# A third unit of the second chunk by 32x32 squares and VectorE transposes, with its loads and the loads of v on GpSimd's queue

## The chip, the cores and the metric

The program runs on one core of a Trainium2 chip. The metric is the device time in microseconds (us). Three timed runs of the kernel before gave 600.76, 600.92 and 600.96 us; their median is 600.92 us. One further execution was profiled; it took 601.11 us, of which the profile's span covers 599.4 us.

Engines are named as in the profile: PE (TensorE matmuls), PEld (its weight loads), DVE (VectorE), ACT (ScalarE), POOL (GpSimd), SP (SyncE, which here only issues DMAs).

## The reference

Two parts, one after the other. The first is a gated linear recurrence per head (4 batches, 8 heads, 768 time steps, head size 48), the second a SwiGLU block over 3072 tokens.

```python
f = 1.0 / (1.0 + np.exp(-f_logit))            # q, k, v, f_logit: (4, 8, 768, 48) float32
state = np.zeros((B, H, D, D))
for t in range(S):
    state = f[:, :, t, :, None] * state + einsum('bhd,bhe->bhde', k[:, :, t], v[:, :, t])
    y[:, :, t] = einsum('bhd,bhde->bhe', q[:, :, t], state)
x = y.transpose(0, 2, 1, 3).reshape(3072, 384)
g = x @ w_gate                                # 384 x 1536, float64 in memory
out = (g * sigmoid(g) * (x @ w_val)) @ w_out  # w_out: 1536 x 384
```

The weights arrive as float64 (two 32-bit words per element) and are turned into float32 on the chip.

## The kernel before

**Units.** The sequence is cut into six chunks of 128 steps. A unit is one batch of one chunk; `units` counts them chunk by chunk, so units 0 to 3 are the four batches of chunk 0, units 4 to 7 those of chunk 1, and so on to 23. For one unit, `attention(u)` (L556) is a generator that yields between pieces of work. With products of gates along the chunk it makes a scaled k (`kT`) and a scaled q (`qT`), both with the head dimension on partitions; scores `sc` = kT by qT (L668), masked into `A` (L683); the output `y` from `A` with v and from `qT` with the state that came in; and the update `dS` of the state from the transposed scaled k (`kt`) with v (L749).

**Two ways to bring a unit into that layout.** f, k and q lie in memory with time first. For the early units they are loaded as rows of time (`raw`, two slots of each kind) and turned on PE: four 128x128 transposes each for f (`fTp`, L601), k (`kTp`, L628) and q (`qTp`, L629), and four more to get `kt` (L670 to 672), which ACT copies out of PSUM (L681). For later units, those for which `by_squares(u)` (L401) holds, the loads put the data into `rooms` as 32x32 squares, four DMAs for each of f, k and q (L445 to 449), and DVE transposes the squares (L605, L616, L654). `kt` is then made in one of two ways; in chunk 1 it is turned by DRAM: DVE transposes the squares of `kT` into the room of k (L638), four DMAs write that to a scratch tensor in DRAM (L641), and one DMA reads it back in another order as `kt` (L679). In the first two chunks the rooms are the same memory as the two raw slots together (L399), and these DMAs are on GpSimd's queue; L451 and L452 keep their order on POOL.

Before the change `by_squares` holds from unit 6 on. So units 4 and 5 of chunk 1 go by PE and units 6 and 7 by squares.

**Loads.** `load(u, what)` (L431) issues them. f, k, q and v of units 0 to 5 are on SP's queue, as are the 18 weight pieces of 768 KB (L472), which wait for one of four buffers `w64`. v of units 6 and 7 and the squares are on POOL's queue. v has four slots in the first two chunks; the load of unit u waits until unit u-4 has used its slot. `load_ahead` (L1227) loads the raw units 2 to 4, the v of the next unit and one weight piece in turn; the load of unit 5 with all four inputs is at L1270, those of unit 6 follow from L630 (when unit 5's k and q have been transposed), those of unit 7 from `load_after` inside unit 6.

**Order of the work.** From 0 to about 30 us the four units of chunk 0 run one behind the other. Then PE works on the SwiGLU block of chunk 0 (`mlp_plain`, gate and val products L804, then the down products `o` L827), with the 16 steps of chunk 1's units between them: `attention_steps` (L766) sorts them, and `take_turns` (L1192) deals them out over the pieces of the block. DVE converts weights meanwhile (`join`, L497 to L502), multiplies `h` by val (L818), and forms sums of weights (`extra` and `w_both`, L907 and L910). Up to L1273 the order on PE, DVE, ACT and SP is the order of the code (`in_order`); POOL is not in that list. From there to L1300, about 45 to 130 us, the order on each engine is chosen when the program is built, from which work is ready and which was written first. From about 141 us on, chunks 1 to 5 of the block run as fifteen products (`mlp_fifteen`) with the remaining units by squares between them, again in the order of the code; the change leaves the code of that stage alone.

Of the kernel before, what the change touches and what calls it, by code (L numbers as in the profile page):

```python
# [290 lines left out]
def short_path(ctx, tc, ident, least, judge, q, k, v, f_logit, moe_w_gate, moe_w_val, moe_w_out, out):  # L291
# [9 lines left out]
    nc = tc.nc  # L301
    B, H, S, D = q.shape
# [13 lines left out]
    SQUARES = 2  # L316
# [82 lines left out]
    rooms = {nm: t.rearrange("p n h w -> p (n h w)")[:, 0:Q + HP * RUN] for nm, t in both_raw.items()}  # L399

    def by_squares(u):  # L401
        return u >= SQUARES * B - 2

    def make_rooms(pool):
        for nm in "fkq":
# [3 lines left out]
    def v_of(u):  # L409
        return vs[u % (NV if units[u][1] < SQUARES else NV // 2)]  # L410
# [20 lines left out]
    def load(u, what="fkqv"):  # L431
        b, c = units[u]
        rows = slice(c * C, (c + 1) * C)
        inputs = dict(f=f_logit, k=k, q=q, v=v)
        for nm in "fqkv" if c >= SQUARES else "fvkq" if by_squares(u) else "fkqv":
            src = inputs[nm]
            if nm not in what:
                continue
            if nm == "v":
                dst = v_of(u)  # L440
            elif not by_squares(u):
                dst = raw[nm][u % NRAW]
            else:
                since = len(traced)
                for n in range(4):  # L445
                    at = Q * (1 - n % 2)
                    (nc.sync if c >= SQUARES else nc.gpsimd).dma_start(
                        out=rooms[nm][Q * n:Q * (n + 1), at:at + HP * RUN].rearrange("t (a e) -> t a e", a=HP),
                        in_=src[b, n // 2::2, rows, :].rearrange("a (t i) d -> t a (i d)", i=NI))
                if c < SQUARES:  # L450
                    by_pool.extend(ins for ins in traced[since:] if ins.engine == mybir.EngineType.Pool)  # L451
                    keep_order(by_pool[-5:])  # L452
                continue
            queue = nc.gpsimd if c < SQUARES and by_squares(u) else nc.sync
            queue.dma_start(out=dst[:, :, 0:D], in_=src[b, :, rows, :].rearrange("h t d -> t h d"))

    def weight_piece(dst, src, parts):
# [98 lines left out]
    def attention(u):  # L556
# [70 lines left out]
        if not in_squares:  # L627
            kp = transposed("kTp", kr)  # L628
            qp = transposed("qTp", qr)  # L629
            if by_squares(u + 1):  # L630
                load(u + 1)
# [120 lines left out]
        if c >= SQUARES and u + 2 < len(units):  # L752
            load(u + 2, "v")
# [7 lines left out]
    def load_after(u, what):  # L761

        if u + 1 < len(units) and u + 1 != SQUARES * B:
            load(u + 1, what)
# [16 lines left out]
    def keep_order(mine):  # L781
        for a, b in zip(mine, mine[1:]):
            tc.add_manual_dep(b, a.name, mybir.DependencyInfo(mybir.DependencyClass.NoSync,
                                                              mybir.DependencyReason.DATA), reason="order")
# [418 lines left out]
    def weights():  # L1203
        if fetches:
            fetches.pop(0)()
        if sizes:
            sizes.pop(0)()
        if joins:
            joins.pop(0)()
# [57 lines left out]
    joins.pop(0)()  # L1267
    hidden[1]()
    weights()
    load(B + 1)  # L1270
    hidden[2]()
    steps.pop(0)()
    in_order(mark, (mybir.EngineType.PE, mybir.EngineType.DVE, mybir.EngineType.Activation, mybir.EngineType.SP))  # L1273
# [66 lines left out]
def kernel(  # L1340
# [22 lines left out]
    def judge(bank):  # L1363
# [13 lines left out]
        yield  # L1377

    short_path(tc, ident, least, judge, *args)
    with tc.If(redo[0] > 0, label="redo"):  # L1380
        general_path(tc, *args)
# [32 lines left out]
```

## Time and profile before

| what | value |
|---|---|
| median of three runs | 600.92 us (600.76 to 600.96) |
| the profiled execution | 601.11 us |
| its span | 599.4 us |
| PE busy | 588.3 us, 98% of the span |
| DVE busy | 481.8 us, 80% |
| ACT busy | 293.5 us, 49% |
| POOL busy | 93.8 us, 16% |
| granted TensorE clock of the core | 0.998 |

The page gives for each engine the busy time and then, in 40 slices of 15 us, the busy share in tenths. A row of a timeline has the start in us, the duration in us, the engine, the line of the code, the operation, what it writes and reads, and how many such instructions were merged; brackets give the idle time of that engine before it and what ended it. PE's matmuls are pipelined, so the room that a matmul takes is best read from one start to the next. A row of windows gives each engine's busy time in a stretch. A row of the DMA view gives, for one queue, the packets, the megabytes, and the time the packets took as a share of the 16 DMA engines' time; q1 is SP's queue, q0 is GpSimd's.

### The profile page before, as it was taken

To read this page: it belongs to the slowest core of one execution; us is meant where nothing else is said; L and a number is where in the kernel's file an instruction comes from. 1 tells how busy PE (TensorE), PEld (TensorE's weight loads), DVE (VectorE), ACT (ScalarE), POOL (GpSimd) and SP (SyncE) were. 2 spreads that over 40 slices of the span, in tenths; PEclk is the share of its full clock that TensorE was granted. 3 is DMA by queue.
4 is the path that set the end of the run, shared out by engine and by line. 5 is a ranking of instruction groups with operands and counts; after the bars stand their busy time and mean duration, and the time that the engine had idled before them with its cause. 6 is when DMAs were issued, how large, how long until landed. Compare 5 with 4: busy or idle time off the path is not lost.

```text
span 599.4 us, 10861 instructions
## 1 busy us (share of the span) xinstructions
PE 588.3 (98%) x3996; PEld 485.3 (81%) x3996; DVE 481.8 (80%) x833; ACT 293.5 (49%) x557; POOL 93.8 (16%) x211
## 2 busy tenths in 40 slices
PE   7899999999999999999999999999999999999996
PEld 5744545667888899888899888899988899988896
DVE  7999998978999977998995978995878972666731
ACT  2577854115776422576740576632376730356600
POOL 1102235100030240121130030320030320000000
PEclk9999999999999999999999999999999999999999
DMA  9998664124331144442344422343230100100001
GB/s 199 262 284 296 191 191 116 24 70 141 81 79 53 47 113 113 129 101 67 102 115 103 130 75 69 97 113 98 81 103 26 28 10 6 54 1 2 1 1 55
DMA packets 104058, 57.33 MB, mean 96 GB/s; under 512 B 65632, under 2 KB 95712, under 8 KB 104000
## 3 DMA queue, kind: packets, MB, share of 16 engines
q1 hardware_dynamic: 95552, 46.09, 29.2%
q0 software_dynamic: 6432, 7.75, 4.5%
q10 hardware_dynamic: 2016, 2.75, 1.3%
q8 instruction: 32, 0.52, 0.4%
q14 instruction: 26, 0.21, 0.1%
HBM read 46.27 MB, written 7.34 MB: 89 GB/s over the span
## 4 chain that ended last, share of the span: by engine, by line
PE 97%; DVE 1%; ACT 0%; issue 0%; DVEq 0%; ACTq 0%
PE o L1105 20%; PE A L1006 18%; PE B L1006 14%; PE c L1006 6%; PE o L1006 6%; PE o L827 5%; PE gate L804 5%; PE val L804 5%; PE sc L668 4%; PE o L1168 3%; PE y L708 3%; PE y L729 2%; PE dS L749 2%; PE y L704 1%; PE kt L672 1%; PE fTp L591 0%
## 5 line engine op out<-in xcount | busy, mean ns | idle before, releaser
L719 POOL DMA_DIRECT2D xT<-yT x120 | 59.7, 506 | 50.1 <-ACT yT L712 45.2
L1006 PE MATMUL A<-xs,w_both 128*128 128x256 f32 x240 | 62.2, 382 | 0.0
L1105 PE MATMUL o<-w_out,h 128*128 128x192 f32 x360 | 62.0, 327 | 0.0
L1105 PEld LDWEIGHTS o<-w_out,h 128*128 128x128 f32 x360 | 58.7, 190 | 1.2 <-DVE h L958 0.3
L1011 ACT COPY c<-A 128x512 f32<-128x512 f32 x40 | 23.3, 583 | 60.8 <-PE A L1006 60.8
L1011 ACT COPY aside<-A 128x512 f32<-128x512 f32 x60 | 35.1, 585 | 34.1 <-PE A L1006 34.0
L907 DVE TENSOR_TENSOR c<-c,aside 128x512 f32<-128x512 f32 x60 | 41.1, 686 | 12.6 <-ACT aside L1011 11.1
L1006 PEld LDWEIGHTS A<-xs,w_both 128*128 128x128 f32 x240 | 44.9, 190 | 6.6
L958 DVE TENSOR_TENSOR h<-h,c 128x256 f32<-128x256 f32 x100 | 40.5, 413 | 7.6 <-ACT h L1022 7.3
L683 DVE TENSOR_TENSOR A<-sc,causal 128x512 f32<-128x512 f32 x48 | 31.0, 686 | 15.7 <-PE sc L668 15.7
L910 DVE TENSOR_TENSOR c<-c,aside 128x512 f32<-128x512 f32 x60 | 40.9, 682 | 2.5 <-ACT aside L1011 2.5
L1022 ACT ACTIVATE h<-c 128x256 f32<-128x256 f32 x100 | 39.2, 416 | 6.6 <-DVE c L907 5.1
L1105 PE MATMUL o<-ws,h 128*128 128x192 f32 x240 | 41.5, 328 | 0.2 <-DVE A L683 0.2
L1006 PE MATMUL B<-xs,w_both 128*128 128x256 f32 x160 | 41.2, 380 | 0.0
L1006 PE MATMUL A<-xs,extra 128*128 128x256 f32 x160 | 41.2, 380 | 0.0
L1006 PE MATMUL B<-xT,extra 128*128 128x256 f32 x160 | 41.1, 379 | 0.0
L1006 PE MATMUL c<-xT,w_both 128*128 128x256 f32 x160 | 41.1, 379 | 0.0
L658 POOL MEMSET gates<- 128x4 f32 x24 | 2.6, 110 | 244.7 <-DVE qT L571 239.0
L1105 PEld LDWEIGHTS o<-ws,h 128*128 128x128 f32 x240 | 39.1, 190 | 0.8 <-DVE A L683 0.4
L1011 ACT COPY aside<-B 128x512 f32<-128x512 f32 x60 | 35.1, 584 | 8.3 <-PE B L1006 7.1
L907 DVE TENSOR_TENSOR c<-c,o 128x384 f32<-128x384 f32 x15 | 8.3, 552 | 36.1 <-PE o L1105 36.1
L910 DVE TENSOR_TENSOR c<-o,c 128x512 f32<-128x512 f32 x40 | 27.4, 685 | 11.9 <-ACT h L1022 6.2
(153 smaller groups left out, 1224.3 us busy)
## 6 DMA issues: line engine op xcount, KB each, us to landing
fsquares<-in_f_logit_dram SPq DMA_DIRECT2D x64, 96.0 KB, 2.5
qsquares<-in_q_dram SPq DMA_DIRECT2D x64, 96.0 KB, 2.2
ksquares<-in_k_dram SPq DMA_DIRECT2D x64, 96.0 KB, 2.4
w<-in_moe_w_gate_dram SPq DMA_DIRECT2D x6, 768.0 KB, 5.8
w<-in_moe_w_val_dram SPq DMA_DIRECT2D x6, 768.0 KB, 6.0
w<-in_moe_w_out_dram SPq DMA_DIRECT2D x6, 768.0 KB, 6.1
v<-in_v_dram SPq DMA_DIRECT2D x22, 192.0 KB, 2.9
out_dram<-ob ACTq DMA_DIRECT2D x14, 192.0 KB, 2.0
```

The source lines that it names most:

```text
L668: nc.tensor.matmul(sc[par][:, a * C:(a + 1) * C], lhsT=kT[r, a, :], rhs=qT[r, a, :], start=True, stop=True)
L683: nc.vector.tensor_tensor(A[:, par], sc[par].rearrange("p (a t) -> p a t", t=C), causal.unsqueeze(1).broadcast_to((128, HP, C)), ALU.mult)
L719: (nc.gpsimd if c >= SQUARES else nc.sync).dma_start(out=xT[c][f % 128:f % 128 + n, f // 128, b * C:(b + 1) * C], in_=yT[r:r + n, par, a / ...
L804: nc.tensor.matmul(p, lhsT=w[:, j, i, :], rhs=xT[c][:, i, :], start=(i == 0), stop=(i == KT - 1))
L827: nc.tensor.matmul(p, lhsT=hidden_tile(h, n // 2)[:, n % 2 * 2 + b // 2, b % 2 * C:(b % 2 + 1) * C], rhs=w_out[:, j, :], start=(n == 0), s ...
L907: nc.vector.tensor_tensor(dst, a, b, ALU.add)
L910: nc.vector.tensor_tensor(dst, a, b, ALU.subtract)
L958: lagging.append(lambda: f(*args))
L1006: nc.tensor.matmul(p[name][:, n, :], lhsT=weights_of[a][:, n, j, :], rhs=tokens[b], start=fresh and n == 0, stop=True, skip_group_check=True)
L1011: nc.scalar.copy(t, p[name])
L1022: nc.scalar.activation(dst, src[:, 0, :], AF.Silu)
L1105: nc.tensor.matmul(p[:, n, :], lhsT=lhsTs[j][:, n * C:(n + 1) * C], rhs=rhs[:, j, :], start=first and j == order[0] and n == 0, stop=j == ...
```

## The change

`by_squares` now holds from unit 5 on. Unit 5 so loses its 16 PE transposes and ACT's copy of `kt`, and gets the DVE transposes of f, k and q, the DVE transpose of `kT`, four DMAs to DRAM and one back, and 12 loads of squares in place of three loads of rows. The load of unit 5 at L1270 is removed; in its place L630, inside unit 4, now sees that the next unit goes by squares and loads all four inputs of unit 5 there. Unit 6 is then loaded piece by piece by `load_after` from inside unit 5. In `load`, the rule for the queue becomes: v of units 1 to 7 on GpSimd's queue, everything else that is loaded as rows on SP's. So v of units 1 to 5 moves from SP's queue to GpSimd's.

```diff
     def by_squares(u):
-        return u >= SQUARES * B - 2
+        return u >= SQUARES * B - 3
...
-            queue = nc.gpsimd if c < SQUARES and by_squares(u) else nc.sync
+            queue = nc.gpsimd if nm == "v" and 0 < u < SQUARES * B else nc.sync
             queue.dma_start(out=dst[:, :, 0:D], in_=src[b, :, rows, :].rearrange("h t d -> t h d"))
...
     hidden[1]()
     weights()
-    load(B + 1)
     hidden[2]()
     steps.pop(0)()
```

## The prediction

> **What bounds the kernel now.** I read the page's busy times first, then windows over the stage that the change touches, then timelines of that stage and of the first 12 us, and last the DMA queues.
>
> ```profile
> PE 588.3 (98%) x3996; PEld 485.3 (81%) x3996; DVE 481.8 (80%) x833; ACT 293.5 (49%) x557; POOL 93.8 (16%) x211
> ...
> DMA  9998664124331144442344422343230100100001
> ```
>
> PE has work for all but 11 us. The second line shows the DMA engines full for the first 45 us. Four windows cover the time in which chunk 1's units run beside the first block:
>
> ```profile
> 30.00:56.00 26.00, 26.00 (x86) 12.67 (x87) 25.18 (x45) 18.84 (x26) 1.00 (x2) 1.00 0.92 294
> 56.00:80.00 24.00, 24.00 (x125) 12.63 (x124) 23.79 (x40) 18.47 (x25) 10.27 (x16) 1.00 0.69 208
> 80.00:103.00 23.00, 23.00 (x99) 10.99 (x98) 21.17 (x35) 11.84 (x17) 8.74 (x16) 1.00 0.54 149
> 103.00:130.00 27.00, 27.00 (x214) 17.00 (x213) 20.60 (x35) 4.10 (x8) 3.36 (x6) 1.00 0.13 31
> ```
>
> The columns after the length are busy PE, PEld, DVE, ACT, POOL, then clock, DMA share and GB/s. PE has no gap from 30 to 130 us. So an instruction taken from PE there is worth its whole length, unless PE then waits for something. DVE is the engine to fear: 70.1 of 73 us busy up to 103 us, 20.6 of 27 behind that.
>
> **PE: minus 1.8 us.** Unit 5's transposes in PE's row:
>
> ```profile
> 56.13 0.60 PE L591 MATMUL fTp<-idf,fraw 128*128 128x128 f32 x4
> ...
> 56.56 2.74 PE L804 MATMUL gate<-xT,w_both 128*128 128x512 f32 x6
> ...
> 71.71 0.60 PE L591 MATMUL kTp<-idf,kraw 128*128 128x128 f32 x4
> ...
> 72.15 0.60 PE L591 MATMUL qTp<-idf,qraw 128*128 128x128 f32 x4
> ...
> 72.59 5.32 PE L804 MATMUL val<-xT,w_both 128*128 128x512 f32 x12
> ...
> 78.92 0.66 PE L672 MATMUL kt<-idf,kT 128*128 128x128 f32 x4
> ...
> 79.42 5.32 PE L804 MATMUL gate<-xT,w_both 128*128 128x512 f32 x12
> ```
>
> From start to start, f takes 0.43, k 0.44, q 0.44 and kt 0.50 us: 1.81 us for 16 transposes, some 0.11 us each. That is the most the change can gain in this stage, since PE has no waits there to lose.
>
> **DVE: 3.2 us more, of which I charge 0.4 to the end.** The same operations for units 6 and 7, from 30 to 103 us:
>
> ```profile
> L605 DVE STREAM_TRANSPOSE gates<-fraw 128x512 f32<-128x512 f32 x2 | 2.2, 1104 | 0.0
> ...
> L616 DVE STREAM_TRANSPOSE qT<-kraw 128x512 f32<-128x512 f32 x2 | 1.4, 695 | 0.0
> ...
> L638 DVE STREAM_TRANSPOSE kraw<-kT 128x512 f32<-128x512 f32 x1 | 0.7, 698 | 0.0
> ...
> L654 DVE STREAM_TRANSPOSE tails<-qraw 128x512 f32<-128x512 f32 x1 | 0.7, 673 | 0.0
> ```
>
> One of each: 1.10 + 0.70 + 0.70 + 0.67 = 3.17 us. The multiplications by gates and tails (L571) stay at 0.67 to 0.68 us. If PE becomes 1.8 us shorter as well, DVE has to find 5.0 us. It has 73 - 70.1 = 2.9 us of idle time up to 103 us and 6.4 us from there to 130 us. So it fits in the whole stage but not in its first part. Upper end: 5.0 - 2.9 = 2.1 us of waiting by PE. Lower end: nothing, because DVE works ahead. Unit 7's first DVE operations stand at 94.62 to 100.9 us (transpose 1.09, two scans of 1.2, transpose 0.69 and three small ones, 5.1 us), and their scores run on PE only at 121.42 us. An order chosen anew can put them behind 103 us. A gain is excluded: DVE only gets work. I take 0.4, near the lower end, because 5.1 us of movable work covers the missing 2.1.
>
> [...] The rows of this case, fp32, show 0.11 us on PE and 0.17 to 0.28 us on DVE for each 128x128, so the measured exchange loses DVE almost twice what it frees on PE, and I go by the rows.
>
> **ACT: nothing.** The sigmoid goes from 0.60 us (out of PSUM) to 0.63 us (in place), and the copy of `kt` (0.57 us) disappears. The table loads of 1.28 us around the sigmoid are there either way. ACT has 5.5 us idle between 56 and 80 us; without that cover it would gain 0.5 us.
>
> **Unit 5's loads and its way by DRAM: nothing, with an upper end of 2.2 us.** SP loses three issues (0.44, 0.53, 3.02 us at 32.25 to 36.43 us) and v at 36.48 (0.70); the weight piece behind them at 37.27 us, which ACT awaited for 0.39 us at 43.3, can go once its buffer is free. That gives DVE a few tenths and PE nothing. POOL gets 12 loads at about 0.56 us, 6.7 us, four issues to DRAM (2.91 us at 90.32), one back (0.73). It is 10.27 of 24 us busy at its fullest. The room of f is free when unit 4's f has been transposed at 33 us, those of k and q at 39 us; even at the longest time from first issue to last landing of four such loads (78.35 to 86.78, 8.4 us) all is in by 55 us, and the sigmoid of unit 5 stands at 58.8. Unit 6's f now waits for unit 5's DVE transpose of f, no longer for its PE transpose at 56.56 us. ACT's sigmoid of unit 6 (67.98) has the output copies and a Silu queued behind it; but unit 6's scores are at 104.96, so a later place for the sigmoid costs nothing. Unit 6's k waits for unit 5's turned k to be in DRAM. Between units 6 and 7 that took from 89.33 (L638) to 100.25 (L616), 10.9 us; units 5 and 6 have 27 us between their scores (77.83 and 104.96). The tight one is `kt`: from L638 at 89.33 to its landing at 103.9 unit 6 took 14.6 us, since k and q of unit 7 were issued on POOL before it. Unit 5 needs `kt` for `dS` at 91.33, or 89.5 with PE 1.8 us ahead. If DVE makes `kT` where it does now (76.41 to 77.1), `kt` lands at 91.7 and PE waits 2.2 us. If it makes it before 74.9 us, nothing. The second is likelier: unit 5's k no longer comes from PE at 71.7 to 72.2 but from a load that is in by 55 us.
>
> **v on GpSimd's queue: plus 1.0 us, in the first 30 us.** This is the part that I weigh most. POOL has nothing to do between 3.29 and 10.01 us, and v of units 1 to 3 wait for nothing but the clearing of their slots (2.57 to 3.19). POOL already runs such loads ahead of the code: unit 6's v went out at 24.94 us, before a clearing written much earlier. So I expect the three at 3.3 to 6.4 us, at 0.90 and 1.15 us each as the two at 30.17 and 24.94, and their packets 1.5 to 2.0 us after each issue: from about 5 to 9 us. That collides with unit 1's f:
>
> ```profile
> 3.00 0.71 SPq L455 DMA_DIRECT2D fraw<-in_f_logit_dram  x1
> ...
> 6.60 0.66 PEld L591 LDWEIGHTS fTp<-idf,fraw 128*128 128x128 f32 x4
> ...
> 9.81 1.22 DVE L622 TENSOR_TENSOR_SCAN tails<-gates,floor 128x516 f32<-128x516 f32 x1
> ...
> 10.04 1.16 PE L668 MATMUL sc<-qT,kT 48*128 48x128 f32 x16 [1.24 <-DVE qT L571]
> ```
>
> It lands at 6.56 and PE takes it at 6.60. DVE's scan at 9.81 follows ACT's sigmoid, which ended at 8.14 us, so there is 1.7 us to spare; PE's scores at 10.04 come after that transpose and six idle matmuls, with 1.24 us to spare. How the queues share is seen around unit 6's v, in half-microsecond stretches of the DMA view: 26.5 to 27, and 27.5 to 28.
>
> ```profile
> q1 hardware_dynamic: 603, 0.11, 113.4%
> ...
> q0 software_dynamic: 27, 0.09, 62.6%
> q1 hardware_dynamic: 84, 0.02, 15.7%
> ```
>
> SP's rows go in packets of 192 B, GpSimd's in about 3 KB, and once the latter come, SP's queue falls from 0.11 to 0.02 MB per half microsecond. Three loads of v are 0.59 MB, some 3 us at 0.2 MB/us for both queues; unit 1's f then lands 2 to 3 us later, and PE and DVE start 0.4 to 1.4 us later. Unit 3's f (landed before its transpose at 17.72) gets 0.39 MB of v and then unit 4's v (after 14.8 us) in front of it and may cost up to 0.9 us more. Upper end 2.3 us. Lower end 0: if the three went out a microsecond later, unit 1's f would be through. Below 0 is excluded, because DVE is 9.7 of 10 us busy in both windows from 10 to 30 us and sets the pace, whatever SP saves. I take 1.0, the middle.
>
> [...]
>
> **Sum.** -1.8 + 0.4 + 0 + 1.0 = -0.4 us. The profiled execution (601.11 us, span 599.4 and 1.7 around it) becomes 600.7; it lay 0.19 over the median, so 600.5 for the median. 0.2%, or 1.2 us, is about what a measurement here can tell from no change.
>
> **Rivals.** *All hidden:* the v loads come late enough or share fairly, and DVE's order absorbs its 3.2 us: -1.8, 599.1 us. For it: nothing waits on a DMA in the first 30 us now. Against it: unit 1's f is used 0.04 us after landing. *VectorE becomes the bound:* if the order up to the first down product stays and DVE is 3.2 - 0.75 (its idle time at 81.1) = 2.4 us later there, the last Silu that frees a bank ends at 103.1 in place of 100.7; PE wants that bank at 102.29 - 1.8 = 100.5, and waits 2.6 us: -1.8 + 2.6 + 1.0 = +1.8, 602.7 us. It decides for slower once PE's waiting on DVE passes 2.0 us. For it: `qT` of unit 5 ended at 77.67 us and its scores began at 77.83. Against it: the 5.1 us done ahead. *kt late at dS:* -1.8 + 2.2 + 1.0 = +1.4, 602.3. That the change does not act can't be: unit 5's PE work is left out by a plain condition.
>
> **Numbers.** Forecast 0.44; all hidden 0.24; VectorE the bound 0.22; kt late 0.10. The first is within 0.2%, the second faster, the last two slower. Range: from all hidden (599.1) to VectorE's wait with half the remaining bound of the start (602.7 + 0.6 = 603.3). The likeliest case by itself: 599.8 to 601.9.
>
> **What would show it.** Right: no L591 for unit 5 between 45 and 80 us; four more transposes on DVE, 3.2 us, before 130; v of units 1 to 3 on POOL before 7 us; PE's transpose of unit 1's f at 8 us or later and the first gate product 0.5 to 1.5 us after 29.85; PE without gaps from there to 130. Wrong: v later than 10 us, or a first gate product at 29.9; PE waiting for DVE or for `kt` by more than a microsecond; or an order of DVE that delays a weight piece.

## The result: slower by 0.47%, and the profile after

The changed kernel takes 604.24 us (median of 7 runs, 603.04 to 605.20). The kernel before, run beside it, takes 601.03 us (7 runs, 600.76 to 602.22). The ratio is 1.0047 with a 95% interval of 1.0036 to 1.0058, so the change costs 2.8 us by the ratio and 3.2 us by these medians. The profiled execution took 604.24 us with a span of 602.4 us. In two of the seven executions the mean clock was 1.000; they took 603.04 and 603.05 us. In the other five it was 0.995 to 0.997, and they took 603.45 to 605.20 us. Two executions that lie far from all others, one of the kernel before (2152.72 us) and one of the kernel with idle matmuls in both places (2348.93 us), are left out of every median.

The page's busy times of the changed kernel look almost like those of before: PE is busy half a microsecond less, DVE 2.8 us more.

```profile
PE 587.8 (98%) x3980; PEld 483.4 (80%) x3980; DVE 484.6 (80%) x837; ACT 292.7 (49%) x556; POOL 109.1 (18%) x233
```

The windows over the same four stretches show where it went. The columns are again length, busy PE, PEld, DVE, ACT, POOL, then clock, DMA share and GB/s.

```profile
30.00:56.00 26.00, 26.00 (x86) 12.69 (x87) 25.17 (x45) 20.93 (x29) 10.10 (x18) 1.00 0.92 270
56.00:80.00 24.00, 24.00 (x113) 11.75 (x112) 23.93 (x41) 14.21 (x21) 12.38 (x18) 1.00 0.70 184
80.00:103.00 23.00, 20.71 (x91) 9.57 (x90) 22.08 (x36) 11.97 (x16) 8.53 (x14) 1.00 0.70 212
103.00:130.00 27.00, 26.16 (x141) 16.02 (x142) 22.37 (x38) 4.71 (x10) 3.36 (x6) 0.94 0.16 41
```

PE, which had no gap from 30 to 130 us, now has one of 2.3 us before 103 us and 0.8 us behind it, and its clock in the last window is 0.94 instead of 1.00. PE's timeline of the changed kernel first shows the gain. Behind a `val` product come at once the scores of unit 5, at 76.49 us where they stood at 77.83; the eight transposes that stood at 71.71 to 72.59 us are gone:

```profile
73.82 2.74 PE L804 MATMUL val<-xT,w_both 128*128 128x512 f32 x6
76.49 1.16 PE L668 MATMUL sc<-qT,kT 48*128 48x128 f32 x16
```

And then PE's rows around the first down product, before:

```profile
97.14 5.31 PE L804 MATMUL val<-xT,w_both 128*128 128x512 f32 x12
102.29 2.74 PE L827 MATMUL o<-w_out,h 128*128 128x384 f32 x8
104.96 1.16 PE L668 MATMUL sc<-qT,kT 48*128 48x128 f32 x16
```

and after:

```profile
95.40 5.31 PE L804 MATMUL val<-xT,w_both 128*128 128x512 f32 x12
103.84 4.51 PE L827 MATMUL o<-w_out,h 128*128 128x384 f32 x8 [3.12 <-ACT h L814]
108.27 1.16 PE L668 MATMUL sc<-qT,kT 48*128 48x128 f32 x16
```

In the kernel before, `o` started 5.15 us behind the start of these twelve `val` products. Here PE could have started it at 95.40 + 5.15 = 100.55 us, 1.74 us ahead of the 102.29 of before. It starts at 103.84, a wait of 3.29 us (the row shows 3.12, since the ends of matmuls are modelled). Then the eight `o` products up to the scores of unit 6 take 108.27 - 103.84 = 4.43 us; before they took 2.67 (102.29 to 104.96), so they lose another 1.76 us. The ledger at the scores of unit 6 is -1.74 + 3.29 + 1.76 = +3.31 us, and the first product of `mlp_fifteen` still carries exactly this: 143.89 us against 140.58. All of the loss lies between 100 and 108 us.

What PE waits for is read on ACT and DVE. ACT's timeline, before:

```profile
98.59 0.20 ACT L648 COPY least<-tails 128x4 f32<-128x4 f32 x1 [4.68 <-DVE tails L622]
98.80 1.28 ACT L814 ACT_TABLE_LOAD   x1
100.10 1.09 ACT L814 ACTIVATE h<-gate 128x512 f32<-128x512 f32 x2
```

and after:

```profile
96.05 0.64 ACT L712 COPY yT<-y 128x256 f32<-128x256 f32 x2
101.68 0.20 ACT L648 COPY least<-tails 128x4 f32<-128x4 f32 x1 [4.99 <-DVE tails L622]
101.89 1.28 ACT L814 ACT_TABLE_LOAD   x1
103.19 1.08 ACT L814 ACTIVATE h<-gate 128x512 f32<-128x512 f32 x2
```

The two Silu of 103.19 read the last `gate` products out of the PSUM banks (the memory that PE writes) that `o` needs next; `o` can start when the first of the two, 0.60 us long, is done (103.79 us; it starts at 103.84). The `gate` products were through at about 95.5 us, but the Silu stand behind `least` of unit 7, a copy of 0.20 us, for which ACT sits idle for 4.99 us until DVE's scan of unit 7 is done. The order was the same before, with the scan at:

```profile
97.34 1.21 DVE L622 TENSOR_TENSOR_SCAN tails<-gates,floor 128x516 f32<-128x516 f32 x1
```

DVE's timeline, after:

```profile
99.24 1.09 DVE L605 STREAM_TRANSPOSE gates<-fraw 128x512 f32<-128x512 f32 x1
100.18 0.34 DVE L576 TENSOR_TENSOR decayed<-state,least 128x192 f32<-128x192 f32 x1
100.44 1.21 DVE L622 TENSOR_TENSOR_SCAN tails<-gates,floor 128x516 f32<-128x516 f32 x1
101.68 0.18 DVE L625 RECIPROCAL start<-tails 128x4 f32<-128x4 f32 x1
101.89 1.23 DVE L650 TENSOR_TENSOR_SCAN gates<-gates,start 128x516 f32<-128x516 f32 x1
103.04 0.69 DVE L616 STREAM_TRANSPOSE qT<-kraw 128x512 f32<-128x512 f32 x1
103.81 1.29 DVE L818 TENSOR_TENSOR h<-h,val 128x512 f32<-128x512 f32 x2
```

Unit 7's scan starts at 100.44 us; before it started at 97.34. That is 3.10 us later, which is the 3.17 us of DVE work that unit 5 brings: from 30 us up to that scan DVE is busy 65.53 us before and 68.69 us after, and idle 1.8 us in both. Before, the same copy, table load and first Silu ended at about 100.70 us and PE came at 102.29, so there were 1.59 us to spare. 3.10 later on ACT, 1.74 earlier on PE, less 1.59: a wait of 3.25 us by this sum, 3.29 by the starts in PE's rows.

The second part of the loss is the clock. Windows of 1 us, after:

```profile
102.00:103.00 1.00, 0.00 (x0) 0.00 (x0) 1.00 (x1) 1.00 (x1) 0.00 (x0) 1.00 0.30 113
103.00:104.00 1.00, 0.16 (x1) 0.17 (x2) 0.92 (x3) 0.99 (x3) 0.00 (x0) 0.90 0.39 137
104.00:105.00 1.00, 1.00 (x2) 0.67 (x3) 1.00 (x2) 0.27 (x1) 0.00 (x0) 0.50 0.54 117
105.00:106.00 1.00, 1.00 (x3) 0.41 (x2) 0.10 (x1) 0.00 (x0) 0.00 (x0) 0.50 0.55 110
106.00:107.00 1.00, 1.00 (x3) 0.58 (x2) 0.00 (x0) 0.00 (x0) 0.00 (x0) 0.50 0.00 0
107.00:108.00 1.00, 1.00 (x4) 0.39 (x2) 0.00 (x0) 0.00 (x0) 0.00 (x0) 0.89 0.00 0
```

The granted clock falls to 0.50 behind the gap, in full from 104 to 107 us and in part of the windows on either side (0.90 and 0.89). An `o` product lasts up to 1.01 us meanwhile; in the kernel before each lasted 0.49 us. The gap ahead of this fall is 3.29 us by the starts.

At the start, the timelines of POOL and PE after show that v does go out early and costs little:

```profile
3.23 2.81 POOL L455 DMA_DIRECT2D v<-in_v_dram  x3
```

```profile
7.04 0.66 PE L591 MATMUL fTp<-idf,fraw 128*128 128x128 f32 x4 [0.67 <-DMA fraw<-in_f_logit_dram]
9.89 1.16 PE L668 MATMUL sc<-qT,kT 48*128 48x128 f32 x16 [0.90 <-DVE qT L571]
```

Unit 1's f is transposed at 7.04 us and unit 0's scores begin at 9.89, against 10.04 before. The first `gate` product is at 29.82 us (before 29.85).

### The profile page after: what moved, and what is told of

Its sections match the earlier page's. It is cut to its first block, busy times and chain, and to the rows that moved or that the text cites. A ratio compares the mean times of both kernels' runs of the same rounds, so it can differ in the third digit from the quotient of the medians.

```text
span 602.4 us, 10855 instructions
## 1 busy us (share of the span) xinstructions
PE 587.8 (98%) x3980; PEld 483.4 (80%) x3980; DVE 484.6 (80%) x837; ACT 292.7 (49%) x556; POOL 109.1 (18%) x233
## 4 chain that ended last, share of the span: by engine, by line
PE 82%; DVE 0%; ACT 0%; issue 0%
PE o L1105 20%; PE A L1006 18%; PE B L1006 14%; PE o L1006 6%; PE c L1006 6%; PE o L827 6%; PE sc L668 3%; PE o L1168 3%; PE y L708 2%; PE y L729 1%; PE y L704 1%; PE dS L749 1%; PE kt L672 0%; DVE A L683 0%; ACT h L814 0%; DVE ob L907 0%
## 5 line engine op out<-in xcount | busy, mean ns | idle before, releaser
L907 DVE TENSOR_TENSOR c<-c,aside 128x512 f32<-128x512 f32 x60 | 41.2, 686 | 12.5 <-ACT aside L1011 11.1
L907 DVE TENSOR_TENSOR c<-c,o 128x384 f32<-128x384 f32 x15 | 8.3, 552 | 36.3 <-PE o L1105 36.3
L827 PE MATMUL o<-w_out,h 128*128 128x384 f32 x96 | 34.0, 511 | 3.1 <-ACT h L814 3.1
```

Of the source, the lines that this page charges most:

```text
L827: nc.tensor.matmul(p, lhsT=hidden_tile(h, n // 2)[:, n % 2 * 2 + b // 2, b % 2 * C:(b % 2 + 1) * C], rhs=w_out[:, j, :], start=(n == 0), s ...
L907: nc.vector.tensor_tensor(dst, a, b, ALU.add)
```

## The experiments

The theory to test: DVE's 3.1 us push unit 7's scan back, the scan holds ACT, ACT's Silu hold PE's banks, and the gap on PE in some executions halves the clock behind it. The rivals: the loads of v cost time at the start; or the place of the wait is not DVE's order but DVE's amount of work; or the slow `o` products have nothing to do with the gap.

**One part of the change at a time: the third unit without v's move.**

```diff
-            queue = nc.gpsimd if nm == "v" and 0 < u < SQUARES * B else nc.sync
+            queue = nc.gpsimd if c < SQUARES and by_squares(u) else nc.sync
```

> The changed kernel with v of units 1 to 4 loaded on SyncE's queue again, as before; the third unit by squares stays, with its loads on GpSimd's queue. Theory 1 (VectorE holds ScalarE, and ScalarE's two Silu hold TensorE at the first down product o): the place of the wait lies 90 us behind these loads, so nothing changes: 603.0 to 605.2 us, TensorE waits 3.1 to 3.3 us at o and the granted clock falls to 0.50 behind it. Theory 2 (the loads of v on GpSimd's queue cost time at the start, +1.0 us by the prediction): 1 us less than the changed kernel, 602.0 to 604.2, with the gain visible at the first gate product (29.82 us after, 29.85 before).

Measured: 603.85 us (8 runs, 602.78 to 606.28), ratio to before 1.0049 (1.0031 to 1.0067). The loss is there without v's move. The profiled execution adds something that was not asked for: its clock fell early, at 28 to 31 us, which made PE 1.24 us late from there on (first `gate` product 31.09 us), and the wait at `o` was 2.5 us in place of 3.1. Its line of the waits, `--waits` (what PE waited for: us in total, times, longest):

```profile
PE o L827 <- ACT h L814: 2.5, 1, 2.5
```

A late PE makes the wait shorter: the twelve `val` products ahead of `o` started 1.34 us later than in the changed kernel's profile, the Silu only 0.70 us later (103.89 us). Behind these 2.5 us the clock held (1.00 in every window from 102 to 115 us).

**The other part: v's move on the kernel before.**

```diff
-            queue = nc.gpsimd if c < SQUARES and by_squares(u) else nc.sync
+            queue = nc.gpsimd if nm == "v" and 0 < u < SQUARES * B else nc.sync
```

> The kernel before, with v of units 1 to 7 on GpSimd's queue and nothing else of the change. Theory 1: no step of the chain that ended last in the changed kernel is touched, so 600.8 to 601.4 us, first gate product at 29.8 us. Theory 2 (the prediction's term for the start): +1.0 us, bounds 0 to 2.3: 601.8 to 603.3, with the first gate product at 30.9 us.

Measured: 601.65 us (11 runs, 601.26 to 603.18), ratio 1.001 (1.000 to 1.002). It is 0.6 us, between the two theories. Of it the profile shows 0.12 us: the first `gate` product is at 29.97 us. This makes none of the 3.3 us that the ledger above finds at `o`.

**The order on DVE.** Unit 7's transpose of f has to stand behind the last val multiply that `o` needs. `keep_order` keeps two instructions in the order given; nothing else is changed and no work is taken away.

```diff
-    ahead = set()
+    ahead = set(); vals = []
...
-            nc.vector.transpose(in_turn(pairs(gate)[:, :, 1:N1]), squares("f"))
-            load_after(u, "f")
+            nc.vector.transpose(in_turn(pairs(gate)[:, :, 1:N1]), squares("f")); turned_f = traced[-1]
+            load_after(u, "f"); u == SQUARES * B - 1 and keep_order([vals[-1], turned_f])
...
-            nc.vector.tensor_tensor(part(j), part(j), p, ALU.mult)
+            nc.vector.tensor_tensor(part(j), part(j), p, ALU.mult); vals.append(traced[-1])
```

> The changed kernel, with one order added: unit 7's transpose of f on VectorE (L605), and with it all that needs it (scan L622, L625, L650), stands behind the last of VectorE's val multiplies (L818) that feed the down product, so ScalarE's copy least (L648) of unit 7 stands behind the two Silu that free the banks of gate. The work itself is the same. Theory 1: TensorE comes to o at 100.5 us and waits less than 1 us, the clock stays at 1.0, and nearly all of the 1.74 us saved on TensorE is kept: about 599.3 us (598.8 to 600.5), faster than both kernels, if unit 7's later work (its sc and dS) doesn't come late instead. Theory 3 (the wait at o has another cause: VectorE has 3.1 us more work ahead of o in whatever order, and the val multiplies are late for it too): TensorE waits 2 to 3 us at o all the same, 603 to 604.5 us.

Measured: 600.51 us (11 runs, 599.45 to 602.49), ratio 0.9981 (0.9968 to 0.9994). That is 3.7 us less than the changed kernel, and a little faster than before. ACT's timeline of this kernel:

```profile
97.03 1.28 ACT L814 ACT_TABLE_LOAD   x1
98.33 1.09 ACT L814 ACTIVATE h<-gate 128x512 f32<-128x512 f32 x2
105.06 0.20 ACT L648 COPY least<-tails 128x4 f32<-128x4 f32 x1 [5.65 <-DVE tails L622]
```

The Silu are done at 99.4 us; `least` waits alone, and nobody waits for it. PE's row:

```profile
101.79 2.74 PE L827 MATMUL o<-w_out,h 128*128 128x384 f32 x8
```

No bracket: no wait. `o` starts at 101.79 us and not at 100.55 since in this execution the clock fell at 28 to 31 us too (first `gate` product at 31.06 us, 1.2 us later than in the changed kernel's profile). With the same amount of DVE work in another order the wait is gone: it was the order on DVE, and with it the order on ACT, that made PE wait. ACT's order changed by itself alone was not tried.

**Filling the wait, to part it from the clock.** `keep_warm` issues idle matmuls, whose result nobody reads; here they write a bank of the pool that the units' transposes and outputs use (`aps`), and not one of the banks that the Silu free, so they need not wait for these.

```diff
-                banks.extend(out_bank() for _ in range(B))
+                keep_warm(12, aps, 'a'); banks.extend(out_bank() for _ in range(B))
```

> The changed kernel, with 12 idle matmuls of 128x512 in bf16 (about 0.21 us each, 2.6 us in all) on TensorE just ahead of the first o, where it waits 3.1 us: they fill the wait and compute nothing that is used. Theory 1 in two terms: the wait for the Silu stays (+3.25 us), the fall of the granted clock to 0.50 behind it (+1.76 us on the o products up to sc) goes: 604.2 - 1.8 = 602.4 us (602.0 to 603.0), o x8 up to sc takes 2.7 us instead of 4.43. Rival (the slow o products of the changed kernel come from something other than the gap, for instance from operands that land late): 604 us or more, o x8 still 4.4 us.

Measured: 603.43 us (9 runs, 603.07 to 604.85), ratio 1.0035 (1.0024 to 1.0046): 0.8 us less than the changed kernel, where I expected 1.8. Seven of the nine executions had a mean clock of 0.998 or more and took 603.07 to 603.63 us. The profiled one is of the other two and can't say more: its clock was down to 0.50 from 28 to 34 us, the twelve `val` products started 3.0 us later than in the changed kernel's profile, and the idle matmuls only delayed `o` further (106.11 us, where the first Silu ended at about 105.05, worked out from ACT's busy times). So the early falls of the clock have to be taken out first; that is the kernel with idle matmuls in both places, below.

**The same DVE work on the kernel before.**

```diff
-        nc.vector.tensor_tensor_scan(tail[:, 0:n][:, ::-1], gate[:, 0:n][:, ::-1], floor[:, ::-1], 1.0,
-                                     op0=ALU.mult, op1=ALU.max)
+        [nc.vector.tensor_tensor_scan(tail[:, 0:n][:, ::-1], gate[:, 0:n][:, ::-1], floor[:, ::-1], 1.0,
+                                     op0=ALU.mult, op1=ALU.max) for _ in range(3 if u == B + 1 else 1)]
...
-        multiply(kT, kp, pairs(tail, 2)[:, :, 0:C])
+        [multiply(kT, kp, pairs(tail, 2)[:, :, 0:C]) for _ in range(2 if u == B + 1 else 1)]
```

> The kernel before, with two more scans (L622, 1.22 us each) and one more multiply by the tails (L571, 0.67 us) of unit 5 on VectorE, done again over the same result: 3.1 us more VectorE work at the place where the changed kernel puts its 3.17 us, and nothing else of the change (TensorE keeps all its transposes, no load moves). Theory 1: the two Silu end 3.1 us later than 100.70, so TensorE, which comes to o at 102.3, waits about 3.1 - 1.6 = 1.5 us there, with no fall of the clock after so short a gap: 602.4 us (601.8 to 603.0). Where the wait at o appears but is shorter by some 0.6 to 1.1 us, VectorE's order put a val multiply ahead. Rival (VectorE's added work is hidden and the loss of the changed kernel comes from the loads on GpSimd's queue): no wait at o, 600.8 to 601.2 us.

Measured: 605.38 us (9 runs, 603.86 to 606.92), ratio 1.0063 (1.0043 to 1.0083). It is slower than either theory said, and the place is not the one I named. PE's waits:

```profile
PE sc L668 <- DVE kT L571: 2.7, 1, 2.7
```

I put the load on unit 5's own way to its scores. In the kernel before, the last operand of unit 5's scores (`qT`) ends at 77.67 us, 0.2 us ahead of its use at 77.83, so nearly all of the 3.1 us came out right there, and the scores started at 80.63 us, 2.80 us later. Behind this gap of 2.7 us PE was slower: the four `kt` products took 0.91 us from start to start (82.08 to 82.99), 0.50 in the kernel before (78.92 to 79.42). The granted clock is 0.97 over 40 to 90 us, worth another 1.5 us; it is 1.00 there in the kernel before. The two executions with a mean clock of 1.000 took 603.88 and 603.89 us. The run shows that DVE work on a unit's own tight way comes out nearly in full, but it does not test the wait at `o`.

**A little less DVE work ahead of unit 7's scan.** The third pair of weight sums, 1.28 us at 97.30 us, is asked for a stage later.

```diff
-    for n, at in enumerate((5, 6, 8)):
+    for n, at in enumerate((5, 6)):
...
-    take_turns(hidden + weave(last, sums_of[0][3:7] + sums_of[1][3:7] + sums_of[0][7:] + sums_of[1][7:]), steps, 8)
+    take_turns(hidden + weave(last, sums_of[0][2:7] + sums_of[1][2:7] + sums_of[0][7:] + sums_of[1][7:]), steps, 8)
```

> The changed kernel, with the third pair of the sums of weights (L910, 1.28 us on VectorE at 97.3 us, ahead of unit 7's scan) asked for in the next stage instead. Theory 1: unit 7's scan, least and the two Silu come about 1.3 us earlier, the wait of TensorE at o falls from 3.2 to about 2 us, the clock mostly stays at 1.0: 602 to 602.7 us. Rival (the wait at o is not paced by VectorE's amount of work ahead of unit 7's scan): 603 to 604.5 us with a wait of over 2.8 us.

Measured: 602.81 us (12 runs, 602.11 to 604.24), ratio 1.0023 (1.0011 to 1.0036), 1.4 us less than the changed kernel. But it did not go as theory 1 has it: unit 7's scan did not come earlier (100.73 us against 100.44), since DVE pulled another sum ahead (L907, 0.68 us at 96.03) in place of one of those put off. What changed is ACT's order. One Silu now comes ahead of `least` (98.15 us), so four `o` products can run, and PE waits behind them for the val multiply that stands behind unit 7's work on DVE:

```profile
105.34 1.56 PE L827 MATMUL o<-w_out,h 128*128 128x384 f32 x4 [1.26 <-DVE h L818]
```

The clock fell early in this execution too (first `gate` product 31.02 us), and the twelve `val` products started 2.07 us later than in the changed kernel's profile, so with PE on time the wait would have been longer than 1.26 us. The run speaks for the position in the queues of both DVE and ACT, and says nothing on the amount of work.

**v's move on the kernel with the held order** (on top of the held order).

```diff
-            queue = nc.gpsimd if nm == "v" and 0 < u < SQUARES * B else nc.sync
+            queue = nc.gpsimd if c < SQUARES and by_squares(u) else nc.sync
```

> The kernel with unit 7's f behind the val multiplies (the one that measured 600.51), with v of units 1 to 4 loaded on SyncE's queue again. If the loads of v on GpSimd's queue cost what they cost alone on the kernel before (601.65 against 601.03, +0.6 us, of which its profile shows 0.12): 599.7 to 600.1 us. If they cost nothing and the difference there was the spread of the runs: 600.2 to 600.7 us.

Measured: 600.00 us (12 runs, 599.64 to 602.87), ratio 0.9979 (0.9965 to 0.9992), half a microsecond less than with v on GpSimd's queue, but in both sets single runs lie 2 us above the others, at a mean clock of 0.992. The last experiment takes it up again.

**The early fall of the clock.** In four of the profiles above the clock was at 0.50 for about 3 us or more from 28 us on. Windows of 2 us of the kernel with the held order:

```profile
24.00:26.00 2.00, 1.21 (x28) 1.09 (x28) 1.87 (x3) 1.81 (x5) 1.07 (x2) 1.00 1.01 253
26.00:28.00 2.00, 1.16 (x16) 0.80 (x12) 1.96 (x5) 0.76 (x3) 0.01 (x1) 0.92 1.03 198
28.00:30.00 2.00, 1.84 (x32) 1.52 (x32) 1.93 (x6) 0.78 (x2) 0.00 (x0) 0.50 0.93 349
```

PE is busy for 1.21 + 1.16 of 4 us, in pieces, with no gap over 1.0 us. In the kernel before the same 4 us look the same (1.21 + 1.15 us busy), but the clock holds at 1.00 in the profiled execution. Three idle matmuls in the 0.8 us ahead of unit 3's scores:

```diff
-    run(B - 1, 3)
+    keep_warm(3); run(B - 1, 3)
```

> The kernel that measured 600.51, with 3 idle matmuls (0.21 us each) on TensorE in its idle 0.8 us ahead of sc of unit 3 (24.6 to 25.4 us). In that kernel's profile the granted clock was 0.50 from 28 to 31 us, behind idle stretches of 0.8 and 1.0 us, and the first gate product stood at 31.06 instead of 29.97 (1.1 us). If TensorE's idle share over these few us is what lowers the clock, and the idle matmuls are enough to lift it: the clock stays at 1.0, first gate product at 29.9 to 30.0 us, and the time is 599.4 to 600.2 us with fewer runs above 600.4. If the clock falls for another reason: the same spread, 600.2 to 600.7 us.

Measured: 599.78 us (12 runs, all within 599.46 to 600.30), ratio 0.9974 (0.9963 to 0.9986). The runs above 600.4 are gone. The same windows:

```profile
24.00:26.00 2.00, 1.81 (x30) 1.30 (x31) 1.87 (x3) 1.80 (x5) 1.06 (x2) 1.00 0.84 217
26.00:28.00 2.00, 1.16 (x16) 0.80 (x12) 1.95 (x5) 0.75 (x3) 0.01 (x1) 1.00 1.00 196
28.00:30.00 2.00, 1.83 (x49) 1.37 (x49) 1.93 (x6) 1.29 (x3) 0.00 (x0) 1.00 0.97 331
```

With 0.6 us more of PE work, none of it of use, the clock stays at 1.00. In all 12 executions the mean clock was 0.998 or more; without the idle matmuls 3 of 11 were below that. `o` starts at 100.71 us.

**The control: the same two edits on the kernel before.** The held order in the same lines as above, and

```diff
-    run(B - 1, 3)
+    keep_warm(3); run(B - 1, 3)
```

> The kernel before, with the order that puts unit 7's f behind the val multiplies and with the 3 idle matmuls ahead of sc of unit 3, and nothing of the third unit. In the kernel before TensorE does not wait at o, so the order has nothing to gain there: 600.8 to 601.1 us (the few runs near 602 gone, if the idle matmuls keep the clock up). What the third unit brings when nothing takes it away is then this time less that of the same two edits on the changed kernel (599.78): 1.0 to 1.3 us. Rival (the gain over before of the kernels with the held order comes from the order or the idle matmuls and not from the third unit): 599.8 us here too.

Measured: 600.90 us (11 runs, 600.67 to 601.14), ratio 0.9998 (0.9989 to 1.0007): nothing. So the order and the idle matmuls gain nothing by themselves, and the third unit is worth 600.90 - 599.78 = 1.1 us once its DVE work is out of the way. On PE's timelines the first `o` stands at 100.71 against 102.33 us, 1.62 us; where the other half microsecond is lost again behind it stays open.

**The wait and the clock, parted.** The changed kernel with the 3 idle matmuls at the start only:

```diff
-    run(B - 1, 3)
+    keep_warm(3); run(B - 1, 3)
```

> The changed kernel, with only the 3 idle matmuls ahead of sc of unit 3: the clock stays up in the first 35 us, the wait of 3.1 us at o stays. Theory: 603 us in executions where the clock holds behind that wait, 604.2 to 604.8 where it falls; the median tells how often. First gate product at 29.9 to 30.0 us, wait at o 3.1 to 3.3 us.

Measured: 603.30, 603.33, 604.63, 604.64 and 604.82 us. These are two groups, and the mean clock of the core is 0.999 and 1.000 in the first, 0.995 to 0.997 in the second. The profiled execution is of the first (603.33 us):

```profile
104.49 2.85 PE L827 MATMUL o<-w_out,h 128*128 128x384 f32 x8 [3.54 <-ACT h L814]
107.27 1.16 PE L668 MATMUL sc<-qT,kT 48*128 48x128 f32 x16
```

A gap of 3.5 us, and the clock still held (1.00 in every window from 100 to 140 us): `o` up to the scores takes 2.78 us. Then the same with the 12 idle matmuls ahead of `o` as well:

```diff
-                banks.extend(out_bank() for _ in range(B))
+                keep_warm(12, aps, 'a'); banks.extend(out_bank() for _ in range(B))
...
-    run(B - 1, 3)
+    keep_warm(3); run(B - 1, 3)
```

> The changed kernel with the 3 idle matmuls ahead of sc of unit 3 and the 12 ahead of the first o. The 12 fill 2.6 of the 3.2 us, so the clock holds at o, but o can still not start before the Silu. Theory (the loss is the wait, 3.3 us, and in some executions the clock's fall, up to 1.76 us more): 602.6 to 603.2 us with little spread, o x8 in 2.7 us; less than the kernel with the 3 idle matmuls alone by the clock's share, 0.5 to 1.5 us. Rival (the slow o products are not the gap's doing): o x8 over 4 us here too, and no difference between the two.

Measured: 603.5 us (602.91 to 603.90), ratio 1.0039 (1.0026 to 1.0052), mean clock 0.999 in each of these executions. PE's timeline:

```profile
95.56 5.31 PE L804 MATMUL val<-xT,w_both 128*128 128x512 f32 x12
100.70 2.75 PE L362 MATMUL idle<-floor 128*128 128x512 bf16 x12
104.04 2.85 PE L827 MATMUL o<-w_out,h 128*128 128x384 f32 x8 [0.59 <-ACT h L814]
```

With most of the wait filled none of the five executions has a mean clock as low as the upper group. So the wait costs 3.5 us (603.3 against 599.78 with the held order, same idle matmuls at the start), and the clock another 1.3 to 1.5 us (604.63 to 604.82 against 603.30 and 603.33) in those executions in which it falls. The one profile is of the lower group, so that the clock falls at `o` in the others is inferred: with the same idle matmuls at the start and no wait at `o`, in the kernel with the held order, in the control above and in the next kernel, one of 34 executions was below 0.998; with the wait, three of five.

**v's move again, with the clock steady** (held order, 3 idle matmuls, v of units 1 to 4 on SyncE's queue).

```diff
-            queue = nc.gpsimd if nm == "v" and 0 < u < SQUARES * B else nc.sync
+            queue = nc.gpsimd if c < SQUARES and by_squares(u) else nc.sync
...
-    run(B - 1, 3)
+    keep_warm(3); run(B - 1, 3)
```

> The changed kernel with the held order, the 3 idle matmuls ahead of sc of unit 3, and v of units 1 to 4 back on SyncE's queue. If the move of v costs 0.5 us (601.65 against 601.03 and 600.51 against 600.00): 599.2 to 599.5 us, the fastest of all. If those differences were spread: 599.7 to 600.0 us, like the kernel with v on GpSimd's queue (599.78).

Measured: 599.97 us (11 runs, 599.55 to 600.97), ratio 0.9984 (0.9975 to 0.9993), against 599.78 with v on GpSimd's queue. Here the move costs nothing that can be measured. The half microsecond of the pair above is then more likely the clock's early falls than the move's; the 0.6 us on the kernel before stays unexplained beyond the 0.12 us that its profile shows, and the first `gate` product stands at 30.0 us in this kernel too, with v on SyncE's queue.

| kernel | us | first `o` at, us | wait at `o`, us |
|---|---|---|---|
| before | 601.03 | 102.29 | none |
| before, held order, 3 idle matmuls | 600.90 | 102.33 | none |
| changed | 604.24 | 103.84 | 3.12, clock falls |
| changed, 3 idle matmuls | 603.3 / 604.6 to 604.8 | 104.49 (a run of 603.3) | 3.54, clock holds |
| changed, 3 and 12 idle matmuls | 603.5 | 104.04 | 0.59 |
| changed, held order, 3 idle matmuls | 599.78 | 100.71 | none |

The last row is the version that beats both kernels, by 0.26% (0.14 to 0.37%) over before; that figure counts some executions of before with an early fall of the clock, which the control does not have, and against the control it is 1.1 us or 0.19%.

## Why the prediction was wrong

The forecast of 600.5 us, with a range to 603.3, was 3.7 us low, and the time lies outside the range.

**PE, -1.8 us: right.** -1.74 us at the first `o` of the changed kernel, -1.62 between the two kernels with the held order.

**DVE, the work of 3.17 us: right. The charge of 0.4 us: the step that failed; in its place PE waited 3.29 us.** The charge rested on two covers. One was 2.9 us of idle time up to 103 us; in the changed kernel 1.8 us of it are still idle (25.17 + 23.93 + 22.08 of 73 us are busy), and up to unit 7's scan the idle time did not shrink at all (1.8 us in both kernels): in the changed kernel DVE waits for ACT in 1.4 us of it, and the added work did not go into these holes. The other was "5.1 us of movable work", unit 7's first operations, which an order chosen anew "can put" behind 103 us. It can, and that gains 3.7 us (the held order), but nothing made it do so: unit 7's transpose (99.24 us), scans and `least` (101.68 us) kept their place ahead of the Silu (103.19 us) and the last val multiplies (103.81 us). I asked whether the work could move, not what would move it. The upper end of 2.1 us fell with the same step, since it took all idle time as usable. Both gave a bound on the amount of DVE work, where the loss is one of position. The term "ACT: nothing" has the same fault: it weighs ACT's busy time, and the wait went through ACT's queue.

**The rival "VectorE becomes the bound" named the mechanism and the place:** the Silu that frees a bank (the first of the two, not the last), with 2.6 us of wait. Measured by starts it is 3.29 in the profile; the rows show 3.12 there and 3.54 in another execution. The missing 0.7 us is the idle time "at 81.1" that it subtracted; DVE was idle as long there after the change (0.82 us). I gave it 0.22 because I held the 5.1 us against it. That its 602.7 us lies nearer to the result than the forecast is in part luck: it holds 1.0 us for v that did not come and nothing for the clock.

**The clock: not in the sum at all, +1.76 us in the profiled execution** and 1.3 to 1.5 between groups of runs. A wait of PE was priced at its length only. With it the rival would have come to 604.0 to 604.5 us, above my range.

**v on GpSimd's queue, +1.0 us: wrong in size.** The three loads went out at 3.23 us as foreseen, and unit 1's f was late by 0.43 us (PE's weight load for it went from 6.60 to 7.03 us) and not by 2 to 3, because most of it was through when v's packets came. This stands in the half-microsecond stretches of the DMA view: in the one from 5.5 us SP's queue still had 422 packets against 22; in the next it fell from 630 packets before to 180. There SP's queue kept 0.03 of 0.11 MB, about a quarter; in the stretch that the prediction went by, 27.5 to 28 us of the kernel before, it kept 0.02 of 0.11. PE's reserve of 1.24 us covered the delay: 0 us at the first `gate` product.

**Unit 5's loads and its way by DRAM, nothing: right.** DVE turned `kT` at 62.60 us, `kt` was in at 82.1 us, and `dS` came at 89.60 us with 7.5 us to spare, so the rival of the late `kt` did not arise.

## What to carry to other kernels

Where an order goes by what is ready and what was written first, work that can move need not move: price an addition by what stands behind it in its queue and who waits for that, and pin the order where the answer is bad. Here one line that put unit 7 behind the val multiplies turned a loss of 3.2 us into a gain of 0.5 us, and of 1.2 us with the clock kept up. And a wait of TensorE like these (2.7 to 3.5 us) is to be priced twice, once for its length and once, as a chance, for the clock behind it: 1.3 to 1.8 us where it fell.

## What was not expected of the hardware

The clock's fall is not a matter of the gap's length alone. Behind gaps of 2.48 us (the third unit without v's move) and 3.54 us (3 idle matmuls at the start) it held; behind 2.71 us (more DVE work on the kernel before) and 3.12 us (the changed kernel) it fell, all by the rows of PE. And the same kernel gives both groups of times, with and without a low mean clock (603.3 and 604.6 to 604.8 us). It also fell at 28 us with no gap above 1.0 us, where PE was busy for 2.4 of 4 us; 0.6 us of idle matmuls there cost nothing (600.90 against 601.03 us on the kernel before), and with them in the 12 and 11 runs of two kernels no mean clock was under 0.998; in a third one of 11 was (0.997, 600.97 us). That the low busy share brings the early fall on is what these runs suggest and not proof: profiles with the same busy share held the clock as well (the kernel before, 1.00 with 2.36 of the same 4 us busy). Whether a share of busy time over some stretch decides it was not measured.
